# Decoding raw weights with 16-bit operations, loading the first batch first, and leaving the order up to step 20 to the scheduler

## The chip, the cores and the metric

The kernel runs on one core of one Trainium2 chip. The metric is device time in microseconds (us), the median of three runs. TensorE is called PE, VectorE DVE, ScalarE ACT, GpSimd POOL and SyncE SP, as in the profile. SP issues all transfers here but a few at the very end.

## The reference

```python
def _attn_ref(q, k, v):                  # q, k, v: 8 batches, 8 heads, 576 positions, 64
    q_d, k_d, v_d = (x.reshape(B, H, S // 4, 4, D).mean(axis=3) for x in (q, k, v))
    out_d = softmax_attention(q_d, k_d, v_d)          # 144 x 144 for each head
    out_up = np.repeat(out_d, 4, axis=2)
    mask = np.abs(pos[:, None] - pos[None, :]) < 4    # 7 neighbours
    scores = np.where(mask, scale * q @ k.T, -1e9)
    return out_up + softmax(scores) @ v

def _moe_ref(x, w_in, w_out, alpha):     # x: 4608 x 512
    h = x @ w_in                         # 512 x 2048
    g = np.maximum(h, 0.0) + alpha * np.minimum(h, 0.0)
    return g @ w_out                     # 2048 x 512
```

The attention's output, with the heads side by side, is `x`. The weights and `alpha` come in as float64.

## The kernel before, in words

**Steps.** The two matrix products run over 18 chunks of 256 rows, and each chunk over 8 pairs of 128-column tiles of the hidden layer: 144 steps. Step s has `hidden(s)` (24 matmuls into `h`), `slopes` on ACT, `larger` on POOL in the first 12 steps and on DVE after them, `split` (ACT and POOL make a high part `gh` and a low part `gl`) and `product(s)` (12 matmuls of 512 columns into `o`). Each product of float32 numbers is made of three: high by high, high by low, low by high. So every weight is kept as two tiles, `wih` and `wil` or `woh` and `wol`, in a type that TensorE reads in one pass. Chunks 0, 1 and a quarter of 2 are made of batch 0. `hidden(16)` opens chunk 2, and is the first that needs batch 1.

**Attention.** Batch 0 is made ahead of the steps by `first_batch`, in four pairs of heads. A pair transposes q and k on PE, makes window scores (`fs`) and pooled scores (`fsd`), a softmax of each, and the weighted sums (`fpv`, `fdv`); its last operations write `xh` (L524) and `xl` (L525). The later batches are made beside the steps: `down` makes the pooled part for a pair of heads (POOL folds the loads `ld` into `s2q`, `s2k`, `s2v`), and `local` the neighbours' part for a unit of 192 rows, nearly all of it on DVE. Unit 3 is the first of batch 1.

**Decoding.** A float64 number lies in memory as two 32-bit words, high and low, and these are loaded as they are into `raw`. `make(which, fp, c)` turns a block of them into float32, and then into the high and the low tile; `which` is 0 for w_in and 1 for w_out, and block `fp` is what step fp first needs. Blocks 0 to 5 of each are decoded whole (1024 numbers in each partition, work tile `temp` in SBUF, raw words in three slots), 6 and 7 in halves (512 numbers, `temp` in a bank of PSUM, raw words in tiles that are used for other work later). The w_in blocks are rows of 512, the w_out blocks are multiplied by `sign` as well, which is +1 or -1 for each row. The five operations before are:

- `magnitude`: the absolute value of the high word, read as a float, on ACT (L187)
- `reach`: a clamp (L191), then a shift by 3 and a mask (L192), both on DVE
- `bits`: the sign bit and its neighbour merged in (L196), then the three upper bits of the low word (L197), both on DVE
- `upper`: a rounding copy on ACT (L202, or L206 with `sign`)
- `lower`: the difference on DVE (L210, or L214 with `sign`)

Before the change `N_EARLY` is 5, and blocks 0 to 4 are decoded whole and block 5 in halves.

**What sets the order.** Each engine works its queue in order, and the DMAs stand in SP's queue. For code outside of `tc.manual_schedule()` the compiler's scheduler chooses the order of each queue: among the instructions that it holds ready it takes the one that stands first in the program. Inside of it the written order stays. In the kernel before, `first_batch`, the decoding of blocks below `N_EARLY` and the first pair of `down` are outside. All else is a list of events, each with a time in steps (`at(t, f, ...)`), which is sorted and written out by hand inside `manual_schedule`. The order in which the first loads are written stands in a string, where `a` is q, k and v of a pair, `b` its windows of v, `i` and `o` a block of w_in and w_out:

```python
ORDER = 'i0 a0 a1 b0 o0 a2 b1 a3 b2 i1 b3 o1 i2'
```

Of the kernel before, what the change touches and what calls it, by code (L numbers as in the profile page):

```python
# [11 lines left out]
I32 = mybir.dt.int32  # L12
AF = mybir.ActivationFunctionType
# [12 lines left out]
NF = DF // 128  # L26
# [3 lines left out]
W_MIN = struct.unpack("<f", struct.pack("<I", 0x38000000))[0]  # L30
W_MAX = struct.unpack("<f", struct.pack("<I", 0x47EFFFFF))[0]
# [8 lines left out]
ORDER = 'i0 a0 a1 b0 o0 a2 b1 a3 b2 i1 b3 o1 i2'  # L40
N_EARLY = 5
FIRST = (-1.3, 0.3, 3.4, 6.5)
T0_DEC, D_DEC = 0.5, 0.56
# [8 lines left out]
def tile_attention_moe(ctx: ExitStack, tc: tile.TileContext, q, k, v, w_in, w_out, alpha, out):  # L52
# [57 lines left out]
    gain = const.tile([128, NF], F32, name="gain")  # L110

    def load_alpha():
        nc.sync.dma_start(slope, alpha.rearrange("(f p) -> p f", p=128))
        nc.vector.tensor_scalar(sign, slope, 1.0, 2.0, op0=ALU.is_le, op1=ALU.mult)
        nc.vector.tensor_scalar(sign, sign, -1.0, None, op0=ALU.add)
        nc.vector.tensor_tensor(slope, slope, sign, op=ALU.mult)
# [47 lines left out]
    def make(which, fp, c=None):  # L164
# [6 lines left out]
        def part(i, c):  # L171
            if which == 0:
                return w[i][n][:, 2 * cs[0]:2 * cs[-1] + 2, 256 * half:256 * half + 256]
            f = (2 * fp + c) % 4
            return w[i][n][:, f:f + 1]

        def magnitude():
            if not weights_temp:
# [3 lines left out]
            else:  # L182
                t = bank("ql"[turns[1] % 2], f"temp{which}{fp}{c}").bitcast(I32)
            turns[1] += 1
            st["raw"] = raws[which, fp].pop(c).rearrange("p (k a) b -> p k a b", k=k)
            st["t"] = t.rearrange("p (k a) -> p k a", k=k)
            nc.scalar.activation(f32(st["t"]), f32(st["raw"][:, :, :, 1]), AF.Abs)  # L187

        def reach():
            t = st["t"]  # L190
            nc.vector.tensor_scalar(f32(t), f32(t), W_MIN, W_MAX, op0=ALU.max, op1=ALU.min)  # L191
            nc.vector.tensor_scalar(t, t, 3, 0x3FFFFFF8, op0=ALU.logical_shift_left, op1=ALU.bitwise_and)  # L192

        def bits():
            t, hi, lo = st["t"], st["raw"][:, :, :, 1], st["raw"][:, :, :, 0]
            nc.vector.scalar_tensor_tensor(t, hi, -0x40000000, t, op0=ALU.bitwise_and, op1=ALU.bitwise_or)  # L196
            nc.vector.scalar_tensor_tensor(t, lo, 29, t, op0=ALU.logical_shift_right, op1=ALU.bitwise_or)  # L197

        def upper():
            weight_tiles(which, n)  # L200
            if which == 0:
                nc.scalar.copy(part(0, 0), f32(st["t"]))  # L202
            else:
# [686 lines left out]
    for fp in (NP - 2, NP - 1):  # L890
        at(-1.97, load_raw, 0, fp)
# [98 lines left out]
```

## Time and profile before

| | |
|---|---|
| median of 3 runs | 999.94 us (996.66 to 1003.89) |
| span of the profiled execution | 995.7 us (its own time is not listed beside it) |
| PE busy | 955.8 us, 96% of the span |
| DVE busy | 825.6 us, 83% |
| ACT busy | 559.2 us, 56% |
| POOL busy | 497.8 us, 50% |
| read from HBM | 87.67 MB |

The span runs from the first to the last instruction of one execution. Its 40 slices are 24.9 us each; a digit is the busy share of one in tenths. Shares are means over parts with different limits: the start, with loads, the first batch and decoding, the long middle, and the last 100 us, in which DVE has little left to do. In rows of single instructions the columns are the start, the time from there to the end, engine, line and operation, what is written and read, the count, and in brackets the engine's idle time just before and what ended it. In rows of groups they are the busy time, the mean in ns, and the idle time before.

### The profile page before, as it was taken

To read this page: it belongs to the slowest core of one execution; us is meant where nothing else is said; L and a number is where in the kernel's file an instruction comes from. 1 tells how busy PE (TensorE), PEld (TensorE's weight loads), DVE (VectorE), ACT (ScalarE), POOL (GpSimd) and SP (SyncE) were. 2 spreads that over 40 slices of the span, in tenths; PEclk is the share of its full clock that TensorE was granted. 3 is DMA by queue.
4 is the path that set the end of the run, shared out by engine and by line. 5 is a ranking of instruction groups with operands and counts; after the bars stand their busy time and mean duration, and the time that the engine had idled before them with its cause. 6 is when DMAs were issued, how large, how long until landed. Compare 5 with 4: busy or idle time off the path is not lost.

```text
span 995.7 us, 17954 instructions
## 1 busy us (share of the span) xinstructions
PE 955.8 (96%) x6402; PEld 850.2 (85%) x6402; DVE 825.6 (83%) x1336; ACT 559.2 (56%) x1483; POOL 497.8 (50%) x624
## 2 busy tenths in 40 slices
PE   5977999999999999999999999999999999999998
PEld 4756877888889888888998889898889888899896
DVE  7999887889898889899899888899898889996111
ACT  5766775455656555555565555565556564544442
POOL 2132866677475636555546455655456632324221
PEclk9957999999999999999999999999999999999999
DMA  8947524243423322423322323232324222210000
GB/s 209 217 150 260 159 65 130 79 126 90 131 90 100 111 87 68 136 79 102 98 87 82 117 84 109 91 104 88 100 84 126 85 67 67 70 33 22 1 22 22
DMA packets 63196, 98.27 MB, mean 99 GB/s; under 512 B 23556, under 2 KB 28932, under 8 KB 63108
## 3 DMA queue, kind: packets, MB, share of 16 engines
q1 hardware_dynamic: 62916, 96.88, 33.0%
q8 instruction: 50, 0.82, 0.3%
q10 hardware_dynamic: 192, 0.26, 0.1%
q14 instruction: 38, 0.31, 0.1%
HBM read 87.67 MB, written 9.44 MB: 98 GB/s over the span
## 4 chain that ended last, share of the span: by engine, by line
PE 77%; DVE 12%; ACT 3%; POOL 3%; issue 2%; SPq 1%; DMA 1%; DVEq 0%; POOLq 0%; ACTq 0%
PE o L817 35%; PE h L760 35%; PE s L266 2%; PE pv L300 2%; PE xp L665 1%; DVE temp L196 1%; DVE lb L656 1%; PE pT L290 1%; DVE qk L597 1%; DVE temp L197 1%; DVE ls L601 1%; SPq L399 1%; POOL t L73 1%; DVE wil L210 1%; DVE pv L653 1%
## 5 line engine op out<-in xcount | busy, mean ns | idle before, releaser
L70 POOL TENSOR_TENSOR gl<-t,gh 128x512 fp32r<-128x512 f32 x144 | 186.3, 1294 | 347.2 <-ACT gh L788 340.1
L771 ACT ACTIVATE t<-h,slope 128x256 f32<-128x256 f32 x288 | 136.7, 474 | 144.7 <-PE h L760 117.5
L817 PE MATMUL o<-woh,gh 128*128 128x512 f32 x576 | 194.9, 409 | 2.6 <-ACT sg L823 2.6
L760 PE MATMUL h<-xh,wih 128*128 128x256 f32 x1152 | 189.5, 286 | 0.6 <-ACT xh L524 0.6
L817 PE MATMUL o<-wol,gh 128*128 128x512 f32 x576 | 188.2, 397 | 0.2 <-DVE wol L214 0.2
L817 PE MATMUL o<-woh,gl 128*128 128x512 f32 x576 | 187.9, 397 | 0.0
L760 PE MATMUL h<-xl,wih 128*128 128x256 f32 x1152 | 183.1, 281 | 0.8 <-POOL xl L70 0.8
L760 PE MATMUL h<-xh,wil 128*128 128x256 f32 x1152 | 183.2, 281 | 0.0
L783 DVE TENSOR_TENSOR t<-h,t 128x512 f32<-128x512 f32 x132 | 90.7, 687 | 103.0 <-ACT h L775 101.8
L760 PEld LDWEIGHTS h<-xh,wih 128*128 128x128 f32 x1152 | 163.5, 190 | 11.0 <-issue 1.0
L788 ACT CAST gh<-t 128x512 fp32r<-128x512 f32 x144 | 89.2, 619 | 127.7 <-DVE t L783 95.7
L760 PEld LDWEIGHTS h<-xl,wih 128*128 128x128 f32 x1152 | 156.3, 189 | 1.0 <-POOL xl L70 1.0
L760 PEld LDWEIGHTS h<-xh,wil 128*128 128x128 f32 x1152 | 156.4, 189 | 0.0
L73 POOL TENSOR_TENSOR ld<-ld 72x256 f32<-72x256 f32 x168 | 127.5, 759 | 42.4 <-DMA ld<-in_q 39.7
L601 DVE TENSOR_REDUCE ls<-qk 128x12 f32<-128x768 f32 (+1 forms) x126 | 136.5, 1084 | 3.2
L817 PEld LDWEIGHTS o<-woh,gl 128*128 128x128 f32 x576 | 108.7, 189 | 26.3
L817 PEld LDWEIGHTS o<-wol,gh 128*128 128x128 f32 x576 | 108.3, 188 | 26.4 <-DVE wol L214 1.4
L656 DVE TENSOR_TENSOR lb<-lb,pv 128x384 f32<-128x384 f32 x202 | 113.9, 564 | 5.6
L817 PEld LDWEIGHTS o<-woh,gh 128*128 128x128 f32 x576 | 99.6, 189 | 20.2 <-ACT sg L823 3.1
L775 ACT ACTIVATE h<-h,sign 128x256 f32<-128x256 f32 x264 | 116.1, 440 | 0.0
L653 DVE TENSOR_TENSOR pv<-v,lb 128x1152 f32<-128x1152 f32 x84 | 93.6, 1115 | 2.6
L597 DVE TENSOR_TENSOR qk<-k,qp 128x768 f32<-128x768 f32 (+1 forms) x78 | 83.9, 1076 | 0.0
(151 smaller groups left out, 1133.4 us busy)
## 6 DMA issues: line engine op xcount, KB each, us to landing
k<-in_k SPq DMA_DIRECT2D x41, 384.0 KB
v<-in_v SPq DMA_DIRECT2D x41, 384.0 KB
out<-sg SPq DMA_DIRECT2D x140, 64.0 KB
raw<-in_moe_w_in SPq DMA_DIRECT2D x16, 512.0 KB
raw<-in_moe_w_out SPq DMA_DIRECT2D x16, 512.0 KB
ld<-in_q SPq DMA_DIRECT2D x56, 144.0 KB
ld<-in_k SPq DMA_DIRECT2D x56, 144.0 KB
ld<-in_v SPq DMA_DIRECT2D x56, 144.0 KB
```

Source lines behind the costliest of these rows:

```text
L70: nc.gpsimd.tensor_tensor(o, a, b, op=ALU.subtract)
L73: nc.gpsimd.tensor_tensor(o, a, b, op=ALU.add)
L597: nc.vector.tensor_tensor(st["pr"][:, :nd], window(tiles[u, "k"], half, d0, nd), st["qp", half].unsqueeze(1).to_broadcast([128, nd, 2, 192 ...
L601: nc.vector.tensor_reduce(out=st["s"][:, half, d0:d0 + nd, :].rearrange("p a b -> p (a b)"), in_=st["pr"][:, :nd].rearrange("p a h (t d) - ...
L653: nc.vector.tensor_tensor(st["pr"][:, :nd], window4(tiles[u, "v"], half, d0, nd), prob(half, d0, nd), op=ALU.mult)
L656: nc.vector.tensor_tensor(st["acc"], st["acc"], st["pr"][:, i], op=ALU.add)
L760: nc.tensor.matmul(ph[:, j], w[:, m, 128 * o:128 * o + 128], x[:, m, :], start=(i == 0), stop=(i == 11))
L771: nc.scalar.activation(t[:, j], hs[st][:, j], AF.Copy, scale=slope[:, f:f + 1])
L775: nc.scalar.activation(other[:, j], hs[st][:, j], AF.Copy, scale=sign[:, f:f + 1])
L783: nc.vector.tensor_tensor(gs[st], hs.pop(st), gs[st], op=ALU.max)
L788: nc.scalar.copy(gh, t)
L817: nc.tensor.matmul(outs[c][m], g[:, j, 128 * m:128 * m + 128], wo[w][n][:, o, :], start=(f == 0 and i == 0), stop=(f == NF - 1 and i == 2))
```

## The change: words of 16 bits, loads and order

**Decoding.** The new `make` first writes, in place in `raw`, what the low word is to give: its upper half shifted down by 13 bits into the lower half (`rest_bits`), and the sign bit of the high word into the upper half; for w_out that sign bit is flipped by `turn`, a tile with the sign bit of `sign`. These are operations on 16-bit words at a stride of four. `magnitude` then works in place, scaled by 65536, so that after the clamp (also in place) a shift by 3 drops what has to go, and one operation shifts the high word and merges it with the low one into `temp`. The high tile is a plain copy, the low one a plain difference, for w_out as well.

**Loads.** The first batch's loads are written first, with block 0 of w_in behind its second pair. Block 0 of w_out and block 1 of w_in come after all of the first batch, and the others by events.

**Blocks.** Only block 0 is decoded ahead of the events. Blocks 1 to 5 are decoded whole and 6 and 7 in halves, all of them by events at new times.

**Order.** Events before step 20 are written in the same sorted order, but outside of `manual_schedule`.

```diff
-ORDER = 'i0 a0 a1 b0 o0 a2 b1 a3 b2 i1 b3 o1 i2'
-N_EARLY = 5
+ORDER = 'a0 a1 b0 i0 a2 b1 a3 b2 b3 o0 i1'
+N_EARLY = 1
+WHOLE = tuple((w, fp) for fp in range(N_EARLY, 6) for w in range(2))
+HALVES = tuple((w, fp, c) for w in range(2) for fp in (6, 7) for c in range(2))
-T0_DEC, D_DEC = 0.5, 0.56
+T0_DEC, D_WHOLE, D_HALF, T_LATE = -1.9, 0.5, 0.3, 0.0
+LISTED = 20
...
+        nc.vector.tensor_scalar(turn, sign.bitcast(U16).rearrange("p (n h) -> p n h", h=2)[:, :, 1], 0x8000, None,
+                                op0=ALU.bitwise_and)
...
+        def rest_bits():
+            raw = st["raw"] = raws[which, fp].pop(c)
+            h = raw.bitcast(U16)
+            nc.vector.tensor_scalar(h[:, :, 0], h[:, :, 1], 13, None, op0=ALU.logical_shift_right)
+            if which == 0:
+                nc.vector.tensor_scalar(h[:, :, 1], h[:, :, 3], 0x8000, None, op0=ALU.bitwise_and)
+            else:
+                for i, half in enumerate(cs):
+                    f, r = 2 * fp + half, slice(512 * i, 512 * i + 512)
+                    nc.vector.tensor_scalar(h[:, r, 1], h[:, r, 3], 0x8000, turn[:, f:f + 1],
+                                            op0=ALU.bitwise_and, op1=ALU.bitwise_xor)
...
-            nc.scalar.activation(f32(st["t"]), f32(st["raw"][:, :, :, 1]), AF.Abs)
-
-        def reach():
-            t = st["t"]
-            nc.vector.tensor_scalar(f32(t), f32(t), W_MIN, W_MAX, op0=ALU.max, op1=ALU.min)
-            nc.vector.tensor_scalar(t, t, 3, 0x3FFFFFF8, op0=ALU.logical_shift_left, op1=ALU.bitwise_and)
-
-        def bits():
-            t, hi, lo = st["t"], st["raw"][:, :, :, 1], st["raw"][:, :, :, 0]
-            nc.vector.scalar_tensor_tensor(t, hi, -0x40000000, t, op0=ALU.bitwise_and, op1=ALU.bitwise_or)
-            nc.vector.scalar_tensor_tensor(t, lo, 29, t, op0=ALU.logical_shift_right, op1=ALU.bitwise_or)
+            hi = f32(st["raw"][:, :, 1])
+            nc.scalar.activation(hi, hi, AF.Abs, scale=W_SCALE)
+
+        def bits():
+            raw = st["raw"]
+            hi = f32(raw[:, :, 1])
+            nc.vector.tensor_scalar(hi, hi, W_MIN, W_MAX, op0=ALU.max, op1=ALU.min)
...
+            nc.vector.scalar_tensor_tensor(t, raw[:, :, 1], 3, raw[:, :, 0],
+                                           op0=ALU.logical_shift_left, op1=ALU.bitwise_or)
...
         def lower():
...
+            nc.vector.tensor_tensor(st["l"], f32(st["t"]), f32(st["h"]), op=ALU.subtract)
...
+    at(T_LATE, load_raw, 0, NP - 2)
+    at(T_LATE, load_raw, 0, NP - 1)
+    order = [(w, fp) for fp in range(N_EARLY) for w in range(2)] + list(WHOLE)
+    free = {p: T0_DEC - 0.6 for p in order}
...
+    for w, fp, c in [(w, fp, None) for w, fp in WHOLE] + list(HALVES):
+        d = D_WHOLE if c is None else D_HALF
+        for lag, f in zip((-0.6, -0.3, 0.2, 0.75, 1.0), make(w, fp, c)):
+            at(t + lag * d, f)
+        free[w, fp] = t + 0.3 * d
+        t += d
...
+    for i, p in enumerate(order):
+        if p in WHOLE and p not in raws:
+            at(free[order[i - 3]], load_raw, *p)
...
+    events.sort(key=lambda e: e[:2])
+    for t, _, f, args in events:
+        if t < LISTED:
+            f(*args)
     with tc.manual_schedule():
-        for _, _, f, args in sorted(events, key=lambda e: e[:2]):
-            f(*args)
+        for t, _, f, args in events:
+            if t >= LISTED:
+                f(*args)
```

43 lines of the change are left out of this document (13 added, 30 removed).

## The prediction

> **What bounds the kernel now.** I read the slices of the page first, then the busy time by stretch, then single instructions of PE and DVE in order of time.
>
> ```profile
> PE   5977999999999999999999999999999999999998
> DVE  7999887889898889899899888899898889996111
> ...
> 0.00:37.00 37.00, 25.69 (x172) 22.94 (x172) 29.09 (x60) 21.81 (x54) 5.63 (x26) 1.00 0.93 211
> 37.00:82.00 45.00, 32.11 (x255) 24.75 (x254) 44.67 (x78) 32.78 (x81) 13.51 (x12) 0.60 0.61 188
> 82.00:147.20 65.20, 59.41 (x387) 52.11 (x386) 57.11 (x82) 46.29 (x112) 40.24 (x47) 0.96 0.50 154
> 147.20:191.50 44.30, 41.99 (x269) 36.12 (x268) 34.90 (x54) 23.68 (x69) 29.92 (x37) 0.96 0.40 118
> 191.50:265.00 73.50, 70.37 (x473) 62.70 (x472) 67.66 (x113) 43.51 (x125) 49.99 (x65) 1.00 0.34 100
> 265.00:900.00 635.00, 635.00 (x4282) 570.15 (x4281) 569.06 (x919) 353.41 (x962) 335.85 (x420) 1.00 0.30 91
> ```
>
> In the stretch rows the columns after the length are the busy time of PE, weight loads, DVE, ACT and POOL, then granted clock, DMA share and GB/s. From 265 us on PE has no idle time at all. That part holds steps from 25 on, the change leaves its order by hand (steps from 20) alone, and it lasts as long as before. What can move is when PE gets there: idle PE and work at a clock of 0.60 ahead of 82 us, then 5.8, 2.3 and 3.1 us of idle PE in the next three stretches.
>
> Two chains lead up to that point, and these rows mark them:
>
> ```profile
> 12.66 4.11 PE L451 MATMUL fs<-kT,qb 128*128 128x70 f32 x18
> 49.71 3.95 PE L451 MATMUL fs<-kT,qb 128*128 128x70 f32 x18
> 80.52 0.48 PE L515 MATMUL fpv<-fpT,vw 70*64 70x64 f32 x4 [3.05 <-DVE fxs L518]
> 81.65 0.58 PE L760 MATMUL h<-xh,wih 128*128 128x256 f32 x1 [0.65 <-ACT xh L524]
> ...
> 37.39 0.40 ACT L524 CAST xh<-fxs 128x256 fp32r<-128x256 f32 x1
> ...
> 146.52 0.75 DVE L214 SCALAR_TENSOR_TENSOR wol<-temp,sign,woh 128x512 fp32r<-128x512 f32 x1 [0.76 <-ACT woh L206]
> 147.70 1.34 DVE L597 TENSOR_TENSOR qk<-k,qp 128x1152 f32<-128x1152 f32 x1
> 166.95 0.32 DVE L622 TENSOR_REDUCE lb<-lex 128x12 f32<-128x84 f32 x1 [5.07 <-ACT lex L617]
> 191.55 0.73 PE L760 MATMUL h<-xh,wih 128*128 128x256 f32 x4
> ```
>
> Chain one: the first batch. The steps cannot run before pair 3 of its heads is through, and hidden(0) starts in earnest at 81.65 us, just behind that pair's last cast. Chain two: DVE. It decodes weights until 147.27, takes up unit 3 (second batch) at 147.70, and hidden(16) at 191.55 is the first that reads what unit 3 gives. PE is 91% busy from 82 to 147 (59.41 of 65.20), so neither chain is far ahead of the other; a gain needs both.
>
> **The decode on DVE.** These are the groups up to the end of decoding, and the time of all DVE instructions that touch the tile `temp`:
>
> ```profile
> L196 DVE SCALAR_TENSOR_TENSOR temp<-raw,temp 128x1024 int32<-128x1024 int32 x10 | 13.1, 1308 | 0.1
> L197 DVE SCALAR_TENSOR_TENSOR temp<-raw,temp 128x1024 int32<-128x1024 int32 x10 | 13.2, 1324 | 0.0
> L210 DVE TENSOR_TENSOR wil<-temp,wih 128x1024 fp32r<-128x1024 f32 x5 | 7.1, 1416 | 0.0
> L214 DVE SCALAR_TENSOR_TENSOR wol<-temp,sign,woh 128x512 fp32r<-128x512 f32 x16 | 11.7, 751 | 2.7 <-ACT woh L206 2.6
> L191 DVE TENSOR_SCALAR temp<-temp 128x1024 f32<-128x1024 f32 x10 | 6.9, 688 | 1.9 <-ACT temp L187 1.9
> L192 DVE TENSOR_SCALAR temp<-temp 128x1024 int32<-128x1024 int32 x10 | 6.9, 694 | 0.1
> L196 DVE SCALAR_TENSOR_TENSOR temp<-raw,temp 128x512 int32<-128x512 int32 x12 | 8.2, 687 | 0.0
> ...
> sum 147.20, DVE 93.30 ACT 38.48; mean DVE 31.10 ACT 12.83
> ...
> L196 DVE SCALAR_TENSOR_TENSOR temp<-raw,temp x10: 1196/1215/2169, 10.5 to 90.0; 128x1024 int32<-128x1024 int32 x10
> ```
>
> Before: ten whole blocks at 0.69 + 0.69 + 1.31 + 1.32 + 1.42 (or 2 x 0.75) = 5.4 to 5.5 us, twelve halves, whose temp lies in PSUM, at five operations of about 0.69 = 3.5 us. That is 54.7 + 41.8 = 96.5 us; neighbours overlap a little, so 93.30 were busy, a factor of 0.967.
>
> After: each block has two scalar operations on 16-bit words, one clamp, one merge, one subtraction. No row shows the 16-bit form or a strided result. The nearest is L192, an integer scalar operation of 1024 elements at 0.69; the upper end is one element at a time, the 1.21 of L196; the lower is L192 with half of its streaming time gone, about 0.43. I take 0.69, the row with the same operation and place. The step between 0.69 and 1.21 is 0.52 for 512 elements, so 512 elements come to 0.69 - 0.26 = 0.43. A whole w_in block is 3 x 0.69 + 1.31 + 1.42 = 4.8, a w_out block, whose sign flip takes two operations of 512, 4.97; twelve wholes 58.6. A half is 3 x 0.43 on the raw words in SBUF, and 0.69 each for the merge into PSUM and the subtraction from it: 2.67, eight of them 21.4. Sum 80.0 x 0.967 = 77.4 us, **15.9 less**. With the 16-bit operations at 1.21 (0.69 for halves) 16.1 come back and nothing is saved; at 0.43 (0.69 less half of that 0.52) about 8 more are saved.
>
> The Trainium skill (VectorE: DVE Perf Modes, "What auto-detection actually checks") lets 16-bit data run at four elements a cycle only with a step of one; here the step is four half-words. By it the lower end falls away and two a cycle remains; no run here shows it yet.
>
> **What whole blocks cost beside POOL.** Decoding more as wholes puts two-input operations with both inputs in SBUF beside POOL's work. The trace has one such place:
>
> ```profile
> 90.03 2.17 DVE L196 SCALAR_TENSOR_TENSOR temp<-raw,temp 128x1024 int32<-128x1024 int32 x1
> 92.12 2.29 DVE L210 TENSOR_TENSOR wil<-temp,wih 128x1024 fp32r<-128x1024 f32 x1
> 94.33 2.31 DVE L197 SCALAR_TENSOR_TENSOR temp<-raw,temp 128x1024 int32<-128x1024 int32 x1
> ...
> 89.50:96.60 7.10, 4.64 (x38) 4.39 (x37) 7.07 (x5) 3.75 (x9) 4.51 (x3) 1.00 1.02 365
> ...
> 48.92 0.68 DVE L192 TENSOR_SCALAR temp<-temp 128x1024 int32<-128x1024 int32 x1
> ...
> 48.67 2.65 POOL L73 TENSOR_TENSOR ld<-ld 72x256 f32<-72x256 f32 x1
> ```
>
> Three operations of about 1.2 took 2.2 to 2.3 while POOL worked: 3.2 us lost. In the changed kernel some seven whole blocks, 14 such operations, fall after hidden(0), where POOL is busy 62% of the time (40.24 of 65.20): 14 x 0.62 x 1.0 = 8.7, that is 5.5 more than now (ends: nothing, and 11 if all collide). Net decode: 77.4 + 5.5 = 82.9.
>
> **When decoding ends.** DVE was busy 130.9 us up to 147.2; without decode that leaves 37.6, unchanged. Its idle time was 7.9, 0.3 and 8.1 us in the three stretches. The middle one was already ordered by the scheduler, the last mostly by hand; I let the scheduler bring 8.1 down to 2. Ahead of 37 us there is only one weight block to fill DVE with, so 10 there instead of 7.9. 37.6 + 82.9 + 12 = 132.5: **15 us earlier**. Unit 3 then loses part of its 5.07 us wait for its exponential, which stood behind other ACT work in the written order; I count 2.5, since the scheduler may also fill that gap with less urgent work. Chain two: -17.
>
> ACT does the same absolute value and rounding for each block; the sign is now in the bits, so two casts of 512 become one of 1024. ACT is busy 46.29 of 65.20 there and I cost this at nothing; without that slack it would be some tenths of a us per block. The one 16-element operation for `turn` lies in the first stretch, where DVE is busy 29.09 of 37.00 us.
>
> **When hidden(0) starts.** One weight load fewer lies ahead of pair 3's q and k (o0 goes behind everything of the first batch, i0 behind two pairs):
>
> ```profile
> raw<-in_moe_w_out SPq DMA_DIRECT2D x4, 512.0 KB
> ```
>
> A block is two of these, 1.05 MB, at the 211 GB/s of the first stretch 5 us. Then the chain itself: pair 0 needed 37.39 - 12.66 = 24.7 us from its window scores to its first cast, pair 3 needed 81.65 - 49.71 = 31.9, with decode operations between its hops. With little decoded by then, I give pair 3 the length of pair 0: 7 us. hidden(0) at about 69, -12. Ends: -5 (loads alone), -20 (if the 0.60 clock also goes). Of the 11.2 us of idle PE after 82 us I let 4 go. Chain one: -16.
>
> **Sum.** The later chain counts: -16 to -17. The profiled execution shows a span of 995.7 us; its own time isn't listed, the runs (996.66 to 1003.89, median 999.94) lie 1 to 8 us above the span. Both ends of the span are untouched, so I take the difference over: 999.94 - 17 = **983 us**. The forecast's own range is 975 to 990.
>
> **Rivals.**
>
> Word operations at one element per cycle (the change doesn't bring what its words say). For it: stride of four half-words, no such row. Against: L196 reads raw words with a stride and is no slower at 1.21 than L210's dense best. Decode ends at 132.5 + 16 = 148, chain two keeps only the 2.5: 997 us.
>
> Collisions on both sides. The Trainium skill (SBUF — State Buffer, "Which ops grab the shared pair") has a scalar operation in its two-port mode and any POOL operation shut each other out for the whole instruction. Worked out from rows: 21 more scalar operations in the seven blocks, 0.62 of them waiting half a POOL operation of 1.3 us: 8 us, decode ends at 141, about 991. Against it: L192 at 48.92 kept its 0.68 while the POOL operation beside it took 2.65 (such an operation has a median of 0.74: the row of `ld` further down); POOL paid, and POOL has room. That agrees with the exclusion, not with its price falling on DVE.
>
> SP holds the weights back (this one ends slower). Nine whole blocks must now be loaded through three slots while the `ld` loads of the second batch stand in the same queue.
>
> ```profile
> SPq L152 <- DVE temp L197: 16.3, 4, 7.1
> SPq L148 <- DVE temp L197: 14.2, 3, 7.1
> SPq L235 <- DMA ld<-in_q: 13.3, 2, 7.7
> SPq L235 <- POOL s2q L73: 9.6, 4, 4.2
> SPq L235 <- POOL s2k L73: 4.1, 1, 4.1
> ...
> L73 POOL TENSOR_TENSOR ld<-ld x16: 715/737/2646, 45.5 to 127.2; 72x256 f32<-72x256 f32 x16
> ```
>
> The `ld` waits of 36 to 115 us come to 27.0; every load behind them waits too, those of `q`, `k` and of results included. If all fall ahead of weight loads and nothing is decoded in advance, decode ends at 132.5 + 27 = 159.5, 12 late: 1012 us. It decides once the weights are held back by over 15 us. Against it: DVE idled 0.3 us in 37 to 82 with the same queue, and the scheduler places these loads too.
>
> A longer gain: no idle DVE, pair 3 at 62 us, the 11 us of idle PE gone: 968.
>
> **Chances.** Forecast 0.52, longer gain 0.10, one element per cycle 0.12, collisions 0.11, SP 0.15. A measurement of this kernel can tell about 1% (10 us) from no change. Below 990 lie the forecast and the longer gain: faster 0.62; 0.24 within 1%: one element per cycle, collisions and a near miss; slower 0.14. Eight in ten: from 968, the longer gain, to 1003, which leaves out the worse part of the SP case.
>
> **What would show it.** Right: the 16-bit operations of 1024 elements near 0.69, decode over at 130 to 135 us, hidden(0) at 66 to 72, hidden(16) near 175, PE without idle from 250 on, and the later stretch unchanged. Wrong: 16-bit operations at 1.2; merges and subtractions over 2 us all through the decode; waits of DVE or ACT for raw loads; hidden(0) still near 80; or PE waiting behind an early instruction of another kind in the order the scheduler gave it, which no row of before can show.

## The result: 24 us slower

The changed kernel takes 1024.74 us (1023.8 to 1027.49), the one before, run beside it, 1000.28 (996.66 to 1003.89): a ratio of 1.0248, 95% interval 1.022 to 1.0276. The profiled execution's span is 1022.3 us against 995.7. The forecast was 983, with a range of 968 to 1003.

PE and DVE in the 40 slices of the page of the kernel after, and busy time by stretch (length; PE, weight loads, DVE, ACT, POOL with counts; granted clock, DMA share, GB/s):

```profile
PE   6946669999999999999999999999999999999998
DVE  6989799898689888988989888989898889997111
```

```profile
0.00:37.00 37.00, 26.25 (x193) 24.10 (x194) 26.84 (x61) 20.80 (x55) 5.65 (x26) 1.00 0.88 181
37.00:82.00 45.00, 25.15 (x179) 18.96 (x178) 39.56 (x63) 24.64 (x59) 18.14 (x15) 0.56 0.49 153
82.00:147.20 65.20, 44.48 (x278) 38.59 (x277) 57.89 (x62) 34.64 (x74) 40.83 (x29) 0.75 0.53 180
147.20:191.50 44.30, 39.90 (x253) 34.90 (x253) 40.53 (x56) 28.18 (x76) 27.76 (x31) 0.92 0.31 93
191.50:265.00 73.50, 71.33 (x475) 63.37 (x476) 60.23 (x97) 41.90 (x119) 51.43 (x65) 1.00 0.29 87
265.00:900.00 635.00, 634.24 (x4288) 568.99 (x4287) 567.41 (x918) 356.85 (x980) 342.46 (x432) 1.00 0.31 94
```

Count PE's matmuls up to 265 us: 1378 here, 1556 before, 178 fewer. From 265 to 900 us PE does 6.75 a microsecond in both kernels, so the missing 178 are 26 us. That is the loss, and all of it lies ahead of 265 us: this kernel falls 76 behind between 37 and 82, 109 between 82 and 147, and 16 between 147 and 191; ahead of 37 us it is 21 ahead. PE is idle for 57.9 us up to 265 us, and for 35.4 in the kernel before. These 22.5 us are most of the 26; the rest goes with slower work, at granted clocks of 0.56 and 0.75 between 37 and 147 us where the kernel before had 0.60 and 0.96.

The two chains, in rows of single instructions of PE and DVE, and the last of decoding from the view of the tile `wol` (min, median, max in ns, then first and last start):

```profile
94.56 0.59 PE L768 MATMUL h<-xh,wih 128*128 128x256 f32 x1
...
225.13 0.73 PE L768 MATMUL h<-xh,wih 128*128 128x256 f32 x4
...
167.78 2.22 DVE L605 TENSOR_TENSOR qk<-k,qp 128x1152 f32<-128x1152 f32 x2
...
L223 DVE TENSOR_TENSOR wol<-temp,woh x10: 675/1204/1645, 60.8 to 171.2; 128x1024 fp32r<-128x1024 f32 x6, 128x512 fp32r<-128x512 f32 x4
```

hidden(0) starts in earnest at 94.56 us (81.65 before), decoding ends at 171.9 (147.27), unit 3 is taken up at 167.78 (147.70), hidden(16) at 225.13 (191.55). Both chains are late. hidden(16) comes 33.6 us later, but PE is only 26 us behind by 265 us: not all of that delay reaches the end.

DVE's groups of the decoding (busy us, mean ns, idle time ahead):

```profile
L188 DVE TENSOR_SCALAR raw<-raw 128x1024 uint16<-128x1024 uint16 x12 | 15.9, 1324 | 12.8 <-DMA raw<-in_moe_w_out 9.1 <-DMA raw<-in_moe_w_in 3.7
L213 DVE SCALAR_TENSOR_TENSOR temp<-raw 128x1024 int32<-128x1024 int32 x12 | 15.2, 1270 | 0.0
L194 DVE TENSOR_SCALAR raw<-raw,turn 128x512 uint16<-128x512 uint16 x16 | 14.6, 990 | 0.0
L188 DVE TENSOR_SCALAR raw<-raw 128x512 uint16<-128x512 uint16 x8 | 12.5, 1562 | 0.0
L204 DVE TENSOR_SCALAR raw<-raw 128x1024 f32<-128x1024 f32 x12 | 10.1, 839 | 0.0
L223 DVE TENSOR_TENSOR wil<-temp,wih 128x1024 fp32r<-128x1024 f32 x6 | 8.8, 1474 | 0.0
L190 DVE TENSOR_SCALAR raw<-raw 128x1024 uint16<-128x1024 uint16 x6 | 8.4, 1407 | 0.0
L223 DVE TENSOR_TENSOR wol<-temp,woh 128x1024 fp32r<-128x1024 f32 x6 | 8.0, 1333 | 0.0
L213 DVE SCALAR_TENSOR_TENSOR temp<-raw 128x512 int32<-128x512 int32 x8 | 7.3, 908 | 0.0
```

With four smaller groups (L204 and L190 of 512 elements, 7.1 and 4.3; L223 of 512, 2.8 and 2.7) these are 117.7 us. The same sum in the kernel before is 96.2. Lengths of neighbours overlap a little, so DVE is busy for less than such a sum. The first row also holds what turned out to matter as much: 12.8 us in which DVE stood still in front of a load of raw words. The longest piece, in rows of DVE, ACT and PE:

```profile
99.86 1.48 DVE L223 TENSOR_TENSOR wol<-temp,woh 128x1024 fp32r<-128x1024 f32 x1
108.65 1.30 DVE L188 TENSOR_SCALAR raw<-raw 128x1024 uint16<-128x1024 uint16 x1 [7.31 <-DMA raw<-in_moe_w_out]
109.74 0.92 DVE L533 TENSOR_TENSOR xl<-fxs,xh 128x256 fp32r<-128x256 f32 x1
...
110.70 0.47 ACT L781 ACTIVATE sh<-h,gain 128x256 f32<-128x256 f32 x1 [10.46 <-DVE xl L533]
...
111.96 1.22 PE L768 MATMUL h<-xh,wih 128*128 128x256 f32 x4 [11.02 <-ACT sh L781]
```

DVE is through at 101.3 and waits until 108.65 for a block of w_out. Behind that instruction in its queue stands the first batch's last `xl`; ACT waits for it 10.46 us, and PE waits 11.02 us for ACT. In the kernel before, the first to touch a raw block was ACT's `magnitude`; now it is DVE's `rest_bits`.

### The profile page after: what moved, and what is told of

Read it like the earlier page. It is cut to its first block, busy times and chain, and to the rows that moved or that the text cites. A ratio compares the mean times of both kernels' runs of the same rounds, so it can differ in the third digit from the quotient of the medians.

```text
span 1022.3 us, 17951 instructions
## 1 busy us (share of the span) xinstructions
PE 959.5 (94%) x6402; PEld 854.7 (84%) x6402; DVE 840.8 (82%) x1328; ACT 557.6 (55%) x1474; POOL 518.9 (51%) x624
## 4 chain that ended last, share of the span: by engine, by line
PE 80%; DVE 6%; DMA 5%; POOL 4%; issue 2%; SPq 2%; ACT 0%; POOLq 0%; ACTq 0%; DVEq 0%
PE o L825 37%; PE h L768 36%; DMA ld<-in_q 2%; PE s L274 2%; PE pv L308 2%; DMA raw<-in_moe_w_out 1%; PE xp L673 1%; DVE raw L188 1%; PE pT L298 1%; POOL ld L78 1%; DVE temp L213 1%; POOL gl L75 1%; SPq L407 1%; DVE raw L204 1%; PE qkT L261 1%
## 5 line engine op out<-in xcount | busy, mean ns | idle before, releaser
L75 POOL TENSOR_TENSOR gl<-t,gh 128x512 fp32r<-128x512 f32 x144 | 189.1, 1314 | 349.4 <-ACT gh L796 340.0
L768 PE MATMUL h<-xh,wih 128*128 128x256 f32 x1152 | 192.0, 287 | 11.9 <-ACT sh L781 11.0
L78 POOL TENSOR_TENSOR ld<-ld 72x256 f32<-72x256 f32 x168 | 131.9, 787 | 69.7 <-DMA ld<-in_q 57.2
L825 PEld LDWEIGHTS o<-woh,gl 128*128 128x128 f32 x576 | 108.4, 189 | 27.6 <-POOL gl L75 1.8
```

The lines of the kernel that those rows point to most:

```text
L75: nc.gpsimd.tensor_tensor(o, a, b, op=ALU.subtract)
L78: nc.gpsimd.tensor_tensor(o, a, b, op=ALU.add)
L768: nc.tensor.matmul(ph[:, j], w[:, m, 128 * o:128 * o + 128], x[:, m, :], start=(i == 0), stop=(i == 11))
L825: nc.tensor.matmul(outs[c][m], g[:, j, 128 * m:128 * m + 128], wo[w][n][:, o, :], start=(f == 0 and i == 0), stop=(f == NF - 1 and i == 2))
```

## The experiments

Times are medians. The kernel before, run beside each group, had medians of 1000.2, 1001.0, 1000.7, 999.9 and 999.3 us; ratios are to it.

### The parts alone

**e1**: the kernel before with the new `make` and nothing else.

```diff
-        return magnitude, reach, bits, upper, lower
+        return rest_bits, magnitude, bits, upper, lower     # whole new make, its constants and turn
```

> The kernel before with the new decoding operations alone; loads, blocks and the written order stay. Words theory (the 16-bit operations take 1.31 us for 1024 elements, not 0.69, so decoding got longer): a whole block goes from 5.0 to 5.7 (w_in) or 6.0 us (w_out) undisturbed, ten of them +8, halves within 0.2 us each; with further collisions beside POOL 1008 to 1018, at least half of the 24 us lost. Order theory (what the scheduler wrote up to step 20 stands still on the chip): within 6 us of before, 995 to 1006. Loads theory (weights that come later leave DVE idle): within 6 us of before as well.

Measured: 1032.11 us, ratio 1.0319 (1.0292 to 1.0346). The new word operations alone cost 32 us where the order is written by hand. DVE's groups of the decoding sum to 115.9 us in that run against the 96.2 of the kernel before, and its waits for raw words come to only 1.8 us: with this order it is not the load that DVE stands in front of.

**e2**: the changed kernel with the old `make`.

```diff
-        return rest_bits, magnitude, bits, upper, lower
+        return magnitude, reach, bits, upper, lower         # whole old make, its constants and lags
```

> The changed kernel with the old five decoding operations put back; new loads, blocks and the scheduler's order stay (the next load of a slot is written 0.2 of a block later, behind the old merge). Words theory: at least half comes back, 998 to 1012. Order theory: 1015 to 1030, still losing. Loads theory: 1015 to 1030.

Measured: 1014.74 us, 1.0145 (1.0114 to 1.0176). Ten of the 24 us are the words', 14.5 are in loads, blocks and order. The trace of e2 is of its fastest run, 1007.22 us.

**e3**: the changed kernel, all events by hand.

```diff
-LISTED = 20
+LISTED = -100
```

> The changed kernel with every event inside the hand order again, none left to the scheduler. Words theory: 1015 to 1030. Order theory: 1000 to 1012, the waits of PE for 11 us and of DVE for raw loads gone. Loads theory: 1015 to 1030.

Measured: 1060.29 us, 1.0601 (1.0571 to 1.063). The scheduler's order is not what costs: without it the same events are 35 us slower. PE's waits in that run:

```profile
PE h L768 <- ACT wih L220: 42.1, 6, 11.0
```

PE waits 42.1 us for freshly decoded w_in: the times of the events alone do not keep the weights ahead of the steps.

**e4**: the changed kernel with the loads of before.

```diff
-ORDER = 'a0 a1 b0 i0 a2 b1 a3 b2 b3 o0 i1'
+ORDER = 'i0 a0 a1 b0 o0 a2 b1 a3 b2 i1 b3 o1 i2'
```

> The changed kernel with the order of the first loads of before (five weight blocks among the first batch's loads). Words and order theories: 1018 to 1032. Loads theory: DVE decodes two to three blocks ahead of 40 us again, 1005 to 1013.

Measured: 1027.54 us, 1.0261 (1.0228 to 1.0295). In the changed kernel the loads' order is worth 3 us by the medians, which these runs can't tell from nothing. That didn't hold elsewhere (e12, e14).

**e6**: the kernel before, with events below step 20 left to the scheduler.

```diff
+    for t, _, f, args in events:
+        if t < 20:
+            f(*args)
     with tc.manual_schedule():
         for t, _, f, args in events:
+            if t >= 20:
```

> The kernel before with nothing but the order handed over: events before step 20 to the scheduler; old operations, loads and blocks. The kernel with the old words had still lost 14.5 us. Order theory (it is the scheduler's order): 1006 to 1016. Blocks theory (it is more whole blocks decoded beside POOL, ordered late, and the order by itself is no worse than by hand): 985 to 1002.

Measured: 996.46 us, 0.9954 (0.9933 to 0.9975). The order alone gives 4.5 us. This is the fastest kernel here, level with e18.

### What the word operations take

**e8**: the kernel before, followed by operations on tiles of their own: each form three times alone, then five times beside six POOL additions of 128x512. Only their lengths are read.

```diff
+    nc.vector.tensor_scalar(h[:, :, 0], h[:, :, 1], 13, None, op0=rr)               # L862, step 4
+    nc.vector.tensor_scalar(d[:, 0:2048:2], d[:, 1:2048:2], 13, None, op0=rr)       # L866, step 2
+    nc.vector.tensor_scalar(d[:, 0:1024], d[:, 1024:2048], 13, None, op0=rr)        # L868, dense
+    nc.vector.tensor_scalar(r[:, :, 0], r[:, :, 0], 29, None, op0=rr)               # L870, int32, step 2
```

> The kernel before with a stretch of test operations behind its last hidden matmul, first alone, then beside six additions of 128x512 on POOL; only their durations count. Rate theory: shifts of 1024 16-bit words at a stride of four take 1.3 us alone, dense ones less, the 32-bit strided shift and clamp 0.69. Collision theory: beside POOL all scalar operations in SBUF grow by up to a POOL operation each or hold POOL up, those in PSUM (0.69) don't.

Groups of DVE while POOL is idle (busy us, mean ns):

```profile
L862 DVE TENSOR_SCALAR prb<-prb 128x1024 uint16<-128x1024 uint16 x3 | 3.9, 1297 | 0.1
L875 DVE SCALAR_TENSOR_TENSOR prt<-prb 128x1024 int32<-128x1024 int32 x3 | 3.7, 1226 | 0.1
L866 DVE TENSOR_SCALAR prb<-prb 128x1024 uint16<-128x1024 uint16 x3 | 2.2, 736 | 0.1
L864 DVE TENSOR_SCALAR prb<-prb 128x512 uint16<-128x512 uint16 x3 | 2.2, 735 | 0.1
...
L870 DVE TENSOR_SCALAR prb<-prb 128x1024 int32<-128x1024 int32 x3 | 2.1, 695 | 0.1
...
L868 DVE TENSOR_SCALAR prb<-prb 128x1024 uint16<-128x1024 uint16 x3 | 1.3, 427 | 0.1
```

The same shift of 1024 half-words takes 0.43 us dense, 0.74 at a step of two and 1.30 at the step of four that the change uses. On 32-bit words at the same distance in bytes it takes 0.70.

Lengths beside POOL, from the views of these lines (min, median, max in ns over the three alone and the five beside POOL), and POOL's own:

```profile
L862 DVE TENSOR_SCALAR prb<-prb x8: 1292/1697/2099, 1001.1 to 1029.3; 128x1024 uint16<-128x1024 uint16 x8
...
L870 DVE TENSOR_SCALAR prb<-prb x8: 687/1164/1640, 1011.1 to 1049.3; 128x1024 int32<-128x1024 int32 x8
...
L875 DVE SCALAR_TENSOR_TENSOR prt<-prb x8: 1216/1697/2171, 1015.4 to 1071.6; 128x1024 int32<-128x1024 int32 x8
...
L877 DVE TENSOR_SCALAR prp<-prp x8: 693/699/699, 1019.1 to 1079.6; 128x512 int32<-128x512 int32 x8
...
L887 POOL TENSOR_TENSOR pra<-pra x36: 1260/1583/2128, 1021.8 to 1083.5; 128x512 f32<-128x512 f32 x36
```

Every form with its operands in SBUF grows beside POOL, at most by 0.8 to 0.95 us, and POOL's addition of 1.26 us grows by up to 0.87. The one in PSUM stays at 0.70. So both sides pay, whatever the number of inputs. The Trainium skill (SBUF — State Buffer, "Who interferes with whom", on which ops grab the shared pair) ties this contention of a scalar operation to its two-port mode. The 16-bit form contends here too, though its 1.30 us alone are no faster than the 1.23 of an operation with two inputs.

**e5**: the changed kernel, the low word's shift on 32 bits.

```diff
-            nc.vector.tensor_scalar(h[:, :, 0], h[:, :, 1], 13, None, op0=ALU.logical_shift_right)
+            nc.vector.tensor_scalar(raw[:, :, 0], raw[:, :, 0], 29, None, op0=ALU.logical_shift_right)
```

> The changed kernel with one of the 16-bit operations, the shift of the low word, done as a 32-bit operation of the same strided shape. Rate theory (16-bit words at one element a cycle are the loss): 0.69 instead of 1.31 us for 12 wholes and 0.45 instead of 0.74 for 8 halves, 10 us less on DVE: 1012 to 1018. Collision theory (what counts is that POOL and DVE shut each other out, and the 32-bit form does that too): 1018 to 1026.

Measured: 1019.33 us, 1.0175 (1.0149 to 1.0201): 5 us back. By e8 twelve operations are 0.60 shorter, and eight of half the size by up to half of that: 7 to 10 us of DVE, of which 5 reach the end. In the traces DVE's groups of the decoding sum to 105.3 us, 12.4 fewer, while its waits for raw words grow from 12.8 to 18.8: part of what the shorter operations save turns into waiting for the next load.

**e7**: the changed kernel, the eight halves by the old operations, with their work tile in PSUM from the start.

```diff
-        for lag, f in zip((-0.6, -0.3, 0.2, 0.75, 1.0), make(w, fp, c)):
+        for lag, f in zip((-0.6, -0.3, 0.2, 0.75, 1.0) if c is None else (-0.3, 0.0, 0.4, 0.95, 1.2),
+                          (make if c is None else make_old)(w, fp, c)):
```

> The changed kernel with the old operations, whose work tile lies in PSUM, for the eight half blocks alone; the twelve wholes keep the new ones. Rate theory: undisturbed, a half takes 3.3 us the new way and 3.45 the old way, so 1022 to 1028. Collision theory: only the new halves have their words in SBUF and stand against POOL (up to 3.6 us for an operation of 0.74), so 1010 to 1018.

Measured: 1010.99 us, 1.0098 (1.0069 to 1.0127): 14 us back. The halves come late, and from 82 to 147 us POOL is busy for 40.83 of 65.20 us, where from 37 to 82 it was for 18.14 of 45.00. In the changed kernel three of their operations work on raw words in SBUF (L188 of 512 elements has a mean of 1562 where it takes 735 alone); the old ones were at 0.69 to 0.75 throughout. DVE still waits 12.0 us for raw words in e7, so these 14 us are not that wait.

### Where the version with the old words loses 14.5 us

**e9**: e2 with block 5 in halves again.

```diff
-WHOLE = tuple((w, fp) for fp in range(N_EARLY, 6) for w in range(2))
+WHOLE = tuple((w, fp) for fp in range(N_EARLY, 5) for w in range(2))     # and 5 ahead of 6, 7 in HALVES
```

> The changed kernel with the old word operations (1014.7 us), and in it block 5 of w_in and of w_out decoded as halves again, with their work tile in PSUM, as in the kernel before. Theory 'whole blocks beside POOL': what the new blocks cost is the SBUF work tile, since operations of halves in PSUM do not stretch; four halves are 14.0 us of DVE against 10.9 for two wholes, but three of five operations of a whole stretch by about 1 us each beside POOL, so about 1008 (1004 to 1011). Rival 'late blocks': what costs is that blocks 1 to 4 are made by events beside the first steps instead of ahead of them; block 5 came late in both kernels, so 1013 to 1018.

Measured: 1012.59 us, 1.0113 (1.0082 to 1.0145), 2 us from e2: within what these runs tell apart.

**e10**: e2 with blocks 1 to 4 ahead of the events.

```diff
-N_EARLY = 1
-T0_DEC, D_WHOLE, D_HALF, T_LATE = -1.9, 0.5, 0.3, 0.0
+N_EARLY = 5
+T0_DEC, D_WHOLE, D_HALF, T_LATE = 2.1, 0.5, 0.3, 0.0
```

> The changed kernel with the old word operations (1014.7 us), and in it blocks 1 to 4 ahead of all events in the program again (five early blocks), with block 5 whole by events. Theory 'late blocks': the 18 us between this and the run with the order alone (996.5) go, 997 to 1002. Theory 'whole blocks beside POOL': the scheduler places the early blocks where it finds room whatever their place in the program, and block 5 still stretches, 1006 to 1014.

Measured: 1016.79 us, 1.0159 (1.0135 to 1.0183). Neither theory about the blocks gets back what e2 lost.

**e12**: e6 with the first loads of the change. **e13**: e2 with the first loads of before.

```diff
-ORDER = 'i0 a0 a1 b0 o0 a2 b1 a3 b2 i1 b3 o1 i2'      # e12; e13 the other way
+ORDER = 'a0 a1 b0 i0 a2 b1 a3 b2 b3 o0 i1'
```

> The kernel before with events below step 20 left to the scheduler (996.5 us), and the first batch's loads written first as in the change. Theory 'loads' (a step of the prediction, 5 us): 990 to 993. Theory 'the first batch waits for DVE, not for its loads': 995 to 999.

> The changed kernel with the old word operations (1014.7 us) and with the first loads in the order of before; what stays of the change are the blocks, their times and the scheduler's order. Theory 'late weights': the new order of the loads leaves DVE without weights beside the first batch, which cost 13 us when it alone was added to the run with the order alone (996.5 to 1009.5); 998 to 1004 here. Theory 'blocks': the five blocks by events and the wholes in place of halves are the cost, and the loads change nothing, as with the new word operations: 1010 to 1017.

Measured: e12 1009.53 us, 1.0091 (1.0068 to 1.0113), 13 us slower than e6; e13 1002.5 us, 1.0015 (0.9991 to 1.0039), 12 us faster than e2. With the old words the new order of the loads is 12 of the 14.5 us that e2 lost, and its sign is the reverse of the prediction's. Against e6, 6 us are left for the blocks and their times (e13). The absolute value of a block on ACT, first and last start, in e6 and e12:

```profile
L187 ACT ACTIVATE temp<-raw x22: 622/658/1172, 7.6 to 143.6; 128x512 f32<-128x512 f32 x12, 128x1024 f32<-128x1024 f32 x10
...
L187 ACT ACTIVATE temp<-raw x22: 624/658/1253, 20.6 to 161.4; 128x512 f32<-128x512 f32 x12, 128x1024 f32<-128x1024 f32 x10
```

Decoding begins 13 us later, as it does in e2 against e13 (20.4 and 7.4). Up to 82 us DVE then does 63.69 us of work (22.85 + 40.84) where e6 does 71.88 (27.71 + 44.17): in the stretches of e6 and then of e12

```profile
0.00:37.00 37.00, 24.52 (x151) 21.85 (x151) 27.71 (x57) 20.67 (x49) 5.62 (x26) 1.00 0.93 204
37.00:82.00 45.00, 34.27 (x280) 26.58 (x278) 44.17 (x78) 33.13 (x85) 20.36 (x18) 0.62 0.62 184
...
0.00:37.00 37.00, 26.39 (x161) 23.91 (x161) 22.85 (x50) 17.76 (x44) 5.63 (x26) 1.00 0.90 191
37.00:82.00 45.00, 37.74 (x280) 30.73 (x280) 40.84 (x75) 32.49 (x87) 27.72 (x17) 0.69 0.44 148
```

PE gains a little from it there (441 matmuls against 431, and hidden(0) starts at 81.04 where e6 has it at 84.53), and loses it behind, since decoding ends later: its last subtraction starts at 171.4 us, in e6 at 150.8. The same decoding operations sum to 105.0 us in e12 and to 98.8 in e6, and DVE is idle for 24.1 us up to 147.2 us against 17.9. These 12 us fit the 13: what is put off from the early gaps of the first batch has to be done later, where POOL is busier and the same operations take longer.

**e15**: e6 with the weights still earlier.

```diff
-ORDER = 'i0 a0 a1 b0 o0 a2 b1 a3 b2 i1 b3 o1 i2'
+ORDER = 'i0 a0 o0 a1 b0 i1 a2 b1 a3 b2 o1 b3 i2'
```

> The kernel before with events below step 20 left to the scheduler (996.5 us), and with the weights' first loads still earlier: o0 behind pair 0 and i1 behind its windows, in place of behind pair 1's windows and pair 3. Theory 'late weights' by its other side: DVE's idle time ahead of 37 us falls and part of that comes off the time, 990 to 995. Theory 'the first batch' (the prediction's chain one): its loads come later by up to 5 us and the time goes up with them, 998 to 1002.

Measured: 1003.39 us (995.18 to 1005.04), 1.0022 (0.9994 to 1.005). No gain on this side; in the profiled run, one of the faster ones (997.65), hidden(0) starts at 88.33 where e6 has it at 84.53. With the old words, none of the three orders beats the one of before.

### Why the words cost more than their length

**e14**: e7 with the loads of before.

```diff
-ORDER = 'a0 a1 b0 i0 a2 b1 a3 b2 b3 o0 i1'
+ORDER = 'i0 a0 a1 b0 o0 a2 b1 a3 b2 i1 b3 o1 i2'
```

> The changed kernel with the old word operations for the eight halves (1011.0 us) and with the first loads in the order of before. Theory 'late weights': 996 to 1003. Theory 'the wholes' new word operations bind': at 5.9 us a block where it was 5.4, in place in the raw slots, the weights' decoding fills DVE whenever they come; the loads change nothing, 1008 to 1014.

Measured: 1019.94 us, 1.0184 (1.0136 to 1.0233), slower than both answers. Against e13, the new words in the twelve wholes alone, with their times, cost 17 us. Against e7 the loads of before are 9 us slower here: with the new words in the wholes the new order of the loads gains, as the prediction had it, where with the old words it loses 12. The first operation on a whole block, in e14 and then in e7:

```profile
L190 DVE TENSOR_SCALAR raw<-raw 128x1024 uint16<-128x1024 uint16 x12 | 15.6, 1301 | 17.3 <-DMA raw<-in_moe_w_in 9.2 <-DMA raw<-in_moe_w_out 8.0
...
L190 DVE TENSOR_SCALAR raw<-raw 128x1024 uint16<-128x1024 uint16 x12 | 15.9, 1329 | 12.0 <-DMA raw<-in_moe_w_out 8.5 <-DMA raw<-in_moe_w_in 3.5
```

DVE's groups of the decoding sum to 100.1 us in e14, only 2.3 more than the 97.8 of e13, in which DVE does not wait for raw words at all. There the waits for raw words are ACT's (11.6 us). So most of these 17 us are not the length of the operations; e16 to e18 follow the waiting.

**e16**: e6 with the new words in the ten early wholes only, and their shift on 32 bits.

```diff
+            nc.vector.tensor_scalar(raw[:, :, 0], raw[:, :, 0], 29, None, op0=ALU.logical_shift_right)
...
-        for lag, f in zip((-0.3, 0.0, 0.4, 0.95, 1.2), make(w, fp, c)):
+        for lag, f in zip((-0.3, 0.0, 0.4, 0.95, 1.2), make_old(w, fp, c)):
```

> The kernel before with events below step 20 left to the scheduler (996.5 us), its loads and its blocks, and the new word operations in the ten whole blocks alone, with the low word's shift as one 32-bit operation; the halves keep the old ones. By the durations measured alone a whole is 0.69 + 1.30 + 0.69 + 1.23 + 1.42 = 5.3 us against 5.4. Theory 'rate and collisions': no difference, 994 to 999. Theory 'the words as such' (in place in the raw slots, one more hop between DVE and ACT ahead of the clamp): slots come free later and DVE waits for ACT, 1003 to 1010.

Measured: 1007.8 us, 1.0068 (1.0041 to 1.0095), 11 us slower than e6, although DVE's groups of the decoding sum to 95.2 us here and to 98.8 in e6. Rows of DVE and PE:

```profile
79.26 0.69 DVE L187 TENSOR_SCALAR raw<-raw 128x1024 int32<-128x1024 int32 x1 [7.02 <-DMA raw<-in_moe_w_in]
...
80.47 0.81 DVE L557 TENSOR_TENSOR fp<-fp,frs 128x630 f32<-128x630 f32 x1
...
81.33 1.07 PE L562 MATMUL fpt<-ident,fp 128*70 128x128 f32 x4 [7.42 <-DVE fp L557]
```

DVE is through with the instruction before at 72.24 and stands 7.02 us in front of a block of w_in that is still on its way. Behind it stands `fp` of pair 3, and PE waits 7.42 us for that. In e6 the load's lateness falls on ACT, which has the room:

```profile
ACT temp L187 <- DMA raw<-in_moe_w_in: 10.6, 2, 5.5
...
DVE temp L191 <- ACT temp L187: 6.9, 8, 2.2
```

**e17** and **e18**: the changed kernel and e16, with the absolute value of a whole block taken by ACT first, into the work tile. DVE's clamp comes next, on that tile; the 16-bit operations and the merge stay, and the halves stay as they were. The lines shown are those for whole blocks.

```diff
         def magnitude():
-            nc.scalar.activation(hi, hi, AF.Abs, scale=W_SCALE)
+            nc.scalar.activation(f32(st["t"]), f32(st["raw"][:, :, 1]), AF.Abs, scale=W_SCALE)
...
-            nc.vector.scalar_tensor_tensor(t, raw[:, :, 1], 3, raw[:, :, 0],
+            nc.vector.scalar_tensor_tensor(t, t, 3, raw[:, :, 0],
...
-        return rest_bits, magnitude, bits, upper, lower
+        return magnitude, rest_bits, bits, upper, lower
```

> The changed kernel (1024.7 us), with the absolute value of a whole block taken by ACT first, into the work tile, in place of after the two 16-bit operations and in the raw slot; DVE's clamp of that tile comes next, then the same 16-bit operations and the same merge. DVE has the same number of operations of the same length; only which engine meets the load of raw words first differs. Theory 'DVE waits for the load': DVE's waits for raw words (12.8 us, 7.3 in one piece ahead of the first batch's last xl) go to ACT, which has room, 1010 to 1016. Theory 'rate and collisions alone': the operations are as long as before, 1021 to 1027.

> The run with the new word operations in the ten early wholes only (1007.8 us), with ACT taking the absolute value first in the same way. Theory 'DVE waits for the load': the 7.0 us that DVE waited for a raw block at 72 us, with pair 3 of the first batch behind it, go, and the time is that of the run with the order alone, 995 to 1000. Theory 'rate and collisions': no change, 1004 to 1010.

Measured: e17 1011.29 us, 1.0117 (1.0088 to 1.0146), 13 us back; e18 996.85 us, 0.9961 (0.9936 to 0.9986), 11 us back and level with e6. DVE's first operation on the raw words of a whole block in e17, then in e18, and ACT's wait in e18:

```profile
L192 DVE TENSOR_SCALAR raw<-raw 128x1024 uint16<-128x1024 uint16 x12 | 15.9, 1329 | 2.3 <-DMA raw<-in_moe_w_out 1.6 <-DMA raw<-in_moe_w_in 0.7
...
L191 DVE TENSOR_SCALAR raw<-raw 128x1024 int32<-128x1024 int32 x10 | 7.5, 745 | 5.6 <-DMA raw<-in_moe_w_in 3.7 <-DMA raw<-in_moe_w_out 1.9
...
ACT temp L207 <- DMA raw<-in_moe_w_in: 7.2, 2, 5.6
```

In e17 the 12.8 us of waiting are 2.3, while the decoding groups sum to 116.9 us against 117.7. In e18 they sum to 101.1 us, 5.9 more than in e16, and the kernel is 11 us faster all the same. So it is shown that the same work with ACT at the raw words first gives the 13 and the 11 us back. The clamp and the merge also read other tiles here, but took no less time for it. In e18 the wait moves to ACT. In e17 ACT waits only 1.0 us for raw words; it waits 15.8 us for its work tile, and the loads may be there by then. One hop goes as well: ACT's absolute value no longer stands behind DVE's 16-bit operations, for which it waited 27.2 us in the changed kernel, partly the same wait handed on. That DVE itself waited for an absolute value is in no row there. The runs don't part this hop from the wait for the load.

### Whose fault the late load is

**e11**: the changed kernel, raw words loaded from ACT's queue.

```diff
-                nc.sync.dma_start(dst...
+                nc.scalar.dma_start(dst...
```

> The changed kernel (1024.7 us) with the loads of raw words issued from ACT's queue instead of SP's, so that loads of `ld`, q and k that wait for their buffers no longer stand ahead of them. Theory 'SP holds the weights back' (the slower rival of the prediction): DVE's 12.8 us of waiting for raw words goes and with it the 10.5 us that ACT waits for xl, 1010 to 1016. Theory 'DVE work': the lost time is DVE's longer operations, and the waits for raw words only stand where DVE would otherwise run into POOL: 1020 to 1026.

Measured: 1030.34 us, 1.0295 (1.027 to 1.0319), no gain: 5.6 us slower than the changed kernel. DVE still waits 6.0 us for raw words of w_in, and 6.6 us for ACT's absolute values. That run also moves issues and waits onto ACT, so it neither shows SP's queue to be the cause nor clears it. The trace of the changed kernel says more about the longest piece. In rows of DVE, SP (start and length of the issue) and POOL:

```profile
92.64 1.20 DVE L213 SCALAR_TENSOR_TENSOR temp<-raw 128x1024 int32<-128x1024 int32 x1
...
97.94 0.33 SPq L243 DMA_DIRECT2D ld<-in_k  x1
100.28 1.70 SPq L243 DMA_DIRECT2D ld<-in_v  x2
102.10 0.83 SPq L160 DMA_DIRECT2D raw<-in_moe_w_out  x2
...
88.75 11.50 POOL L78 TENSOR_TENSOR s2q<-ld 72x128 f32<-72x128 f32 x2 [20.25 <-PE qkT L261]
```

The block that DVE waited for until 108.65 was issued at 102.10. Its slot had been free since 93.84, when the merge of the block three before it ended. But the load stood in SP's queue behind loads of `ld`, and SP waited 12.8 us, from 85.1 to 97.9, for the buffer of the first of these. That buffer came free with a POOL addition that took 9.16 us, and a second one took 2.38, where such an addition has a median of 0.46 in the kernel before; meanwhile DVE ran one operation after another, most of them with data in SBUF. In e16 too, the block that was late was issued (72.95) right behind loads of `ld` (69.19 and 72.60). So in this piece SP's queue did hold the load back, by 8.3 us; that another order of that queue would cure it is not shown. DVE's four shorter waits for raw words, 5.4 us together, are not followed here.

## Why the prediction was wrong

The step that failed is "when decoding ends", 132.5 us, in two of its terms: the price of the decoding, and DVE's idle time. Decoding ended at 171.9. Up to then DVE was busy for 148.9 us, about 110.5 of them with decoding, and idle for 23.0: some 27.6 us more decoding than the 82.9 of the forecast, 11.0 more idle time than its 12, and 0.8 of other work.

**The price of a 16-bit operation** (0.69 for 1024 elements, 0.43 for 512) is the term that was furthest off. They take 1.30 and 0.74 alone, and on average 1.35 and 1.1 in the kernel. By the prediction's prices they come to 24.5 us in all; they are 55.7. At their length alone they would be 18 x 1.30 + 28 x 0.735 = 44.0; so 19.5 of the 31 us are the rate, and 11.7 are what they grew by in the kernel, which e8 lets read as contention. The sentence on the upper end (1.21, "16.1 come back and nothing is saved") had the rate nearly right. The Trainium skill (VectorE: DVE Perf Modes, "What auto-detection actually checks") named two elements a cycle for this form; the trace does not agree, since 1024 such elements take as long as an operation with two inputs (1.30 and 1.23) and 1.8 times as long as at a step of two.

**What whole blocks cost beside POOL** was counted for two-input operations only (5.5 us more). It fell on the others: merges and subtractions are 44.8 us, 43.8 by the prediction's lengths, but the clamps are 17.2 against 11.7, and the 16-bit operations grew by the 11.7. The rival "collisions on both sides" had the right operations, and the forecast dropped it because "POOL paid, and POOL has room". e8 shows both paying.

**The scheduler's idle time** ("I let the scheduler bring 8.1 down to 2") is the other term that failed. Idle DVE up to 147.2 us was to be 12; it is 10.2 + 5.4 + 7.3 = 22.9. Ahead of 37 us, 10 was right. The rest is the wait for raw words, which no term of the sum held: the order of the five functions was read for what each costs, not for which engine meets the load first. Putting ACT at the raw words first gave 13 us back (e17).

**The load order** was to bring 5 us and 7 more through the first batch. hidden(0) came at 94.56 where 66 to 72 was named, with decoding still between the hops of pair 3. With the old words the order costs 12 to 13 us (e12, e13); with the new ones in the wholes it gains 9 (e14 against e7), and with the new ones throughout 3, which is within the noise (e4). The step itself held: against the run with the loads of before, hidden(0) comes forward in all four comparisons, to 81.04 from 84.53 (e12, e6), 74.36 from 89.50 (e2, e13), 92.64 from 106.50 (e7, e14) and 94.56 from 105.11 (the change, e4). What failed is what was built on it: the other terms put hidden(0) later than before, and with the old words an earlier first batch did not pay, because the decoding was put off. That ACT costs nothing held for its own work, and missed that its slack had been hiding the loads.

**The order of the scheduler** gains, as forecast: 4.5 us by itself (e6).

**Of the rivals**, "one element per cycle" had the rate nearly right and gave 997: it left out the contention and the wait. "SP holds the weights back" had the right sign and, for the longest piece, the right place: a load of weights stood behind `ld` loads for 8.3 us. Its condition, over 15 us, was not met there, and it did not see that DVE would stand in front of the load, with the first batch behind it. Its time of 1012 us leaves out the price of the words.

**The ledger.** With the loads of before, in steps: order -4 (e6), blocks and their times +6 (e13), words in the wholes +17 (e14), in the halves +8 (e4), and the new loads -3 (the change). Taken in another order the same parts are worth other amounts (the loads +12 in e2 and -9 in e7, the halves 14 in e7), so they are not independent. e7 and e17 together were not run; whether 14 and 13 add up stays open. A shorter decoding does not remove the waiting by itself: in e5, with 12 us less of it, DVE waited 6 us more.

## What to carry to other kernels

When a sequence of operations is rearranged, look first at which engine now stands in front of the load: a wait that a slack engine hid can cost its full length on the engine that bounds, and hold up all that is queued behind it. Price a strided narrow operation from a run of that very form, not from the 32-bit row next to it, and ask of every operation in SBUF what runs on POOL beside it; a work tile in PSUM bought back 14 us here at no saving in operations. Work that fills early gaps should have its data early, even if the first chain then starts later: with the old words that was worth 12 to 13 us. With DVE in place of ACT in front of the loads the answer turned round, so such an order has to be tried anew after each change of the work behind it.

## What the hardware showed

- A 16-bit scalar operation of 1024 elements in SBUF took 0.43 us dense, 0.74 at a step of two and 1.30 at a step of four, a 32-bit one with 8 bytes between its elements 0.70.
- Every DVE form in SBUF that was tried beside POOL's additions grew by at most 0.8 to 0.95 us (0.70 to 1.64, 1.30 to 2.10), and the additions from 1.26 to as much as 2.13; DVE in PSUM stayed at 0.70.
- POOL lost much more in one place of the changed kernel: two additions of 72x128, with a median of 0.46 us in the kernel before, took 9.16 and 2.38 us beside an unbroken row of DVE operations. What held them is not shown.
